# Score blocks in pairs, two fills moved into the written order, and the last output tile in three pieces: one edit to a fused attention and ELU kernel

## The chip, the cores and the metric

The kernel runs on one core of one Trainium2 chip. The metric is device time in microseconds of the whole launch, as the median of several runs. Beside it stands one profiled execution, whose trace gives the times of single instructions from the start of its span. A change of under 0.5% (1.6 us here) can hardly be told from no change.

## The reference

Attention with fixed sparse masks over 8 batches, 8 heads, 576 positions and 64 columns per head, and behind it a two-layer MLP with ELU, all from float32 inputs to a float32 output:

```python
scores = scale * q @ k.T                       # per batch and head, 576 x 576
rel = pos[:, None] - pos[None, :]
local   = (rel >= 0) & (rel < 32)              # heads 0 to 3
strided = (rel >= 0) & (pos % 32 equal)        # heads 4 to 7
attn = softmax(where(mask, scores, -1e9))
x = (attn @ v) as 4608 tokens x 512
h = x @ w_in                                   # 512 -> 2048
g = where(h > 0, h, exp(min(h, 0)) - 1)
out = g @ w_out                                # 2048 -> 512
```

## The kernel before

Positions are dealt out by their remainder modulo 8 (s), so a strided head splits into 8 classes of 72 rows, of which each attends to itself alone; local heads use 6 windows of 96 queries with 128 keys. Tokens keep that order in `xT`, and the stores of the output put them back.

The whole kernel is one list, `ORDER`, written out as a string of some 1380 tokens. Every token calls one small function (the dictionary `run`), which issues a few instructions on one engine. Each engine runs its own instructions in the order of the list, and waits on semaphores for what it needs from others; so the list fixes what stands behind what on each queue. A token is a letter and its arguments, such as `S.2l1.0.12`: batch 2, local heads, pair y = 1, half u = 0, PSUM banks 1 and 2. The eight PSUM banks are also chosen by hand in the tokens. The letters:

- `w` 42 matmuls of zeros (L369); `D` loads by POOL's queue (L230 to L268), which convert float32 to bf16 on the way; `K` casts of the first two strided heads, which SP loads as float32 into `stage` (L375).
- `T` transposes of q or k on PE into a bank for batches 0 and 1 (L388 strided, L391 local), `C`/`c` the copies out of it by ACT or DVE (L399 to L403); `X` a transposing DMA by SP for batches 2 to 7 (L575).
- `S` a score block: 8 (strided) or 6 (local) matmuls with 64-row weights into two banks (L427). `e` its exponential on ACT (L434), `m` the product with the mask on DVE (L441, L447), `O` the product with v, whose extra columns of ones give the sums of the softmax (L490 strided, L497 local; L454 to L475 in batches 0 and 1 with separate matmuls for the sums).
- `n` and `r` logarithm of the sums and exponential of its negative on ACT (L525, L530), `x` the product with it on DVE into `xT` (L555).
- `V` and `W` copies of v on DVE: rows of the previous window (L559), and v of the strided heads between columns of ones (L562).
- `L` the first layer for one 128-row block of h and 512 tokens, four matmuls (L582); in chunk 0 as two halves, `a` (strided heads) and `b` (local heads). `h` exp on ACT (L590), `i` or `j` the clamp to min(e, 1) - 1 on DVE or ACT (L599, L597), `g` the maximum with h on DVE (L610, L608), which also frees the bank.
- `Z` a quarter of the second layer for a tile of 128 tokens, four matmuls (L616). `o` or `q` the copy of the tile to SBUF by ACT or DVE (L622), `t` its two or three stores by SP (L634). The copies share four buffers.
- `Y`/`y` the last tile (7.3) in two halves of 256 columns: matmuls (L642), ACT copies the first half (L655), ACT and DVE share the second (L658, L659); stores by SP and for one piece by ACT.
- `F` fills: the strided mask (`ms`), the window mask (`mk` on POOL, `ml` on DVE).

The order of the work is thus: batch 0's attention, then chunk 0 of the MLP with batch 1's attention among its matmuls, and so on; each chunk of 512 tokens needs the batches that hold them. Before the list runs, SP starts the two `stage` loads, POOL two half loads (qs, ks of batch 0), and DVE clears and fills `zero`, `identity`, `mask_1`, both `vl` tiles, `vsp`, `ones` and the gaps of `kT`.

POOL's loads use eight semaphores in turn, so that the ninth load is issued when the first has landed.

Of the kernel before, what the change touches and what calls it, by code (L numbers as in the profile page):

```python
# [45 lines left out]
D.wo3.0 h.0.1 i.0.7 b.0.0 j.0.11 g.0.7 b.0.6 h.0.0 b.0.12 g.0.10 j.0.1 a.0.15.4 D.qs.2 g.0.11 a.0.9.7
h.0.12 g.0.1 b.0.9 h.0.6 T.1s0.k.2 i.0.12 h.0.9 b.0.15 c.1s0.k a.0.3.1 i.0.6 j.0.9 b.0.3 D.ks.2 g.0.12
h.0.15 T.1l0.k.2 i.0.0 h.0.3 a.0.2.5 g.0.9 C.1l0.k b.0.2 D.vs.2 g.0.6 a.0.5.0 j.0.3 a.0.13.7 g.0.0 h.0.2
b.0.5 j.0.15 g.0.3 b.0.13 j.0.2 g.0.15 S.1s0.1.23 T.1l0.q.6 e.1s0.1 g.0.2 T.1l1.k.1 D.kl.2 T.1l1.q.4
C.1l0.q c.1l1.k S.1s0.0.23 a.0.14.5 h.0.5 m.1s0.1 Z.0.3.0.6 e.1s0.0 c.1l1.q V.1 h.0.13 T.1s1.k.4 i.0.5  # L50
# [657 lines left out]
```

## Time and profile before

| what | value |
|---|---|
| median of 3 runs (lowest, highest) | 315.01 us (314.72, 315.85) |
| the profiled execution | 312.68 us |
| its span, first to last instruction | 310.7 us |
| mean granted TensorE clock | 0.974 |
| PE busy (2330 matmuls) | 299.0 us, 96% |
| ACT busy | 234.5 us, 75% |
| DVE busy | 219.1 us, 71% |
| POOL busy | 79.8 us, 26% |
| loads and stores | 37.59 MB, 121 GB/s mean |

The time of an execution holds some 2 us outside the span. In the profile an engine's line such as "L616 PE MATMUL ... x4" is four instructions of line 616; a bracket behind it is the time that the engine stood idle before and what ended that. PE's durations overlap, so that the distance from one start to the next is what a group costs there. PEld is PE's loading of weights.

### The profile page before, as it was taken

How to read it: one execution, taken by the hardware profiler on the slowest of the kernel's cores; microseconds unless marked ns; L12 is line 12 of the kernel's file. 1: busy time of each engine (PE TensorE's matmuls, PEld its weight loads, DVE VectorE, ACT ScalarE, POOL GpSimd, SP SyncE). 2: the span in 40 equal slices, each digit the busy share in tenths (PEclk: the TensorE clock that was granted, in tenths of full speed). 3: DMA queues.
4: the chain of work that ended last, by engine and by line, in shares of the span. 5: the costliest groups of instructions: out<-in, count | busy, mean ns of one | idle time of the engine just before them, and what ended most of it. 6: DMA issues, size and time to landing. Idle time of an engine off the chain costs nothing.

```text
span 310.7 us, 6213 instructions
## 1 busy us (share of the span) xinstructions
PE 299.0 (96%) x2330; PEld 150.4 (48%) x2330; DVE 219.1 (71%) x422; ACT 234.5 (75%) x421; POOL 79.8 (26%) x107
## 2 busy tenths in 40 slices
...
GB/s 164 188 206 194 207 207 193 165 165 194 165 167 135 129 209 147 133 163 67 126 174 185 122 87 151 169 14 95 36 1 70 0 101 0 37 0 0 40 165 68
DMA packets 106717, 37.59 MB, mean 121 GB/s; under 512 B 88992, under 2 KB 101888, under 8 KB 106688
## 3 DMA queue, kind: packets, MB, share of 16 engines
...
q8 instruction: 18, 0.29, 0.4%
...
## 4 chain that ended last, share of the span: by engine, by line
PE 87%; DVE 4%; ACT 3%; DMA 2%; issue 1%; POOL 1%; ACTq 0%; POOLq 0%
PE ps L616 38%; PE ps L582 38%; PE ps L427 4%; DMA ql<-in_q_dram 2%; PE ps L490 2%; PE ps L497 2%; DVE g L608 1%; PE ps L642 1%; ACT e L434 1%; DVE he L599 1%; DVE g L610 1%; PE ps L391 1%; PE ps L470 1%; ACT ln L525 0%; ACT osb L622 0%
## 5 line engine op out<-in xcount | busy, mean ns | idle before, releaser
L616 PE MATMUL ps<-w_out_sb,g 128*128 128x512 bf16 x560 | 135.6, 380 | 0.0
L582 PE MATMUL ps<-xT,w_in_sb 128*128 128x512 bf16 x576 | 132.0, 379 | 0.0
L590 ACT ACTIVATE he<-ps 128x512 f32<-128x512 f32 x144 | 80.4, 596 | 24.7 <-PE ps L582 24.1
L582 PEld LDWEIGHTS <-w_in_sb 128*128 128x128 bf16 x576 | 54.5, 98 | 63.1 <-issue 0.6
L616 PEld LDWEIGHTS <-g 128*128 128x128 bf16 x560 | 50.4, 98 | 53.8 <-DVE g L610 0.4
L610 DVE TENSOR_TENSOR g<-he,ps 128x512 bf16<-128x512 bf16 x89 | 59.5, 683 | 1.3
L555 DVE TENSOR_TENSOR xT<-ps,ln 64x576 bf16<-64x576 f32 (+1 forms) x64 | 42.9, 678 | 23.9 <-ACT ln L530 22.0
L599 DVE TENSOR_SCALAR he<-he 128x512 bf16<-128x512 f32 x89 | 38.3, 439 | 14.6 <-ACT he L590 13.8
L434 ACT ACTIVATE e<-ps 72x576 bf16<-72x576 f32 (+1 forms) x64 | 39.8, 646 | 7.8 <-PE ps L427 6.8
L525 ACT ACTIVATE ln<-ps 64x576 f32<-64x576 f32 (+1 forms) x64 | 36.7, 582 | 8.3 <-PE ps L497 3.8
L608 DVE SCALAR_TENSOR_TENSOR g<-he,ps 128x512 bf16<-128x512 bf16 x55 | 36.9, 682 | 8.4 <-ACT he L597 8.0
L530 ACT ACTIVATE ln<-ln 64x576 f32<-64x576 f32 (+1 forms) x64 | 39.2, 620 | 1.6
L597 ACT ACTIVATE he<-he 128x512 bf16<-128x512 f32 x55 | 33.8, 628 | 2.7 <-DVE g L610 1.2
L236 POOL DMA_DIRECT2D ql<-in_q_dram x24 | 20.0, 840 | 11.6 <-DMA qTl<-ql 9.6
L441 DVE TENSOR_TENSOR pm<-e,mask_s 72x576 bf16<-72x576 bf16 x32 | 14.4, 449 | 9.6 <-ACT e L434 9.4
L622 ACT COPY osb<-ps 128x512 f32<-128x512 f32 x18 | 10.3, 583 | 13.4 <-PE ps L616 10.4
...
L447 DVE TENSOR_TENSOR pm<-e,mask_l 128x576 bf16<-128x576 bf16 x32 | 14.4, 454 | 6.0 <-ACT e L434 5.6
L622 DVE COPY osb<-ps 128x512 f32<-128x512 f32 x17 | 11.6, 688 | 7.1 <-PE ps L616 6.5
L230 POOL DMA_DIRECT2D vs<-in_v_dram x7 | 4.7, 671 | 39.8 <-DVE vsp L562 38.9
L253 POOL DMA_DIRECT2D vl<-in_v_dram x8 | 10.1, 1259 | 8.0 <-PE ps L497 6.6
L490 PEld LDWEIGHTS <-vsp 72*128 72x128 bf16 x192 | 9.2, 98 | 5.1 <-DVE pm L441 0.2
...
## 6 DMA issues: line engine op xcount, KB each, us to landing
...
```

Of the source, the lines that this page charges most:

```text
L434: nc.scalar.activation(e[0:R], tiles.pop(("S", key, u))[0:R], ACT.Exp, scale=scale)
L525: nc.scalar.activation(t, s_ps, ACT.Ln)
L530: nc.scalar.activation(t, t, ACT.Exp, scale=-1.0)
L555: nc.vector.tensor_mul(dst, o_ps, rc)
L582: nc.tensor.matmul(tiles["h", ch, m], lhsT=w_in_sb[:, c, m * 128:(m + 1) * 128], rhs=xT[:, c, ch * CHUNK:(ch + 1) * CHUNK], start=(c == 2) ...
L590: nc.scalar.activation(e, tiles["h", i[0], i[1]], ACT.Exp)
L597: nc.scalar.activation(e1, e, ACT.Relu, bias=1.0, scale=-1.0)
L599: eng.tensor_scalar(e1, e, scalar1=1.0, scalar2=1.0, op0=ALU.min, op1=ALU.subtract)
L608: nc.vector.scalar_tensor_tensor(dst, e1, -1.0, h, op0=ALU.mult, op1=ALU.max)
L610: nc.vector.tensor_tensor(dst, e1, h, op=ALU.max)
L616: nc.tensor.matmul(ops, lhsT=g[ch % 2][:, m, kk * 128:(kk + 1) * 128], rhs=w_out_sb[:, m, :], start=(m == 0), stop=(m == MC - 1), skip_gro ...
L622: eng(o_sb, tiles.pop(("o", int(ch), int(kk))))
```

## The change

`ORDER` is replaced as a whole: the tokens of the same kinds stand in another order and use other banks. What differs beside place and bank:

- Score blocks (`S`) stand in pairs, one directly behind the other on PE, from batch 2 on: 24 groups of two (30 groups of one to three before). In batches 0 and 1 there are 9 groups (10 before).
- The fill of `vsp` and of the second `vl` tile, which DVE did before the list, become tokens (`F.vp`, `F.v1`).
- The casts of the first strided heads: both of q on ACT, one of k on DVE and one on ACT (both of q on DVE, both of k on ACT before).
- Batch 0: the order of the transposes, of the blocks and of the loads of the weights. The two transposes T.1s1.q and T.1s0.q of batch 1 come later.
- 4 of the 89 clamps of DVE go to ACT; 7 of ACT's 18 output copies go to DVE.
- The last tile in three pieces of 256, 128 and 128 columns; the first copied by ACT, the others by DVE. Tile 8.3 is copied and stored ahead of it, no longer behind it, and tile 7.0 beside its first piece.
- Two small clears more in `kT` (32 columns behind the keys of the local heads).

```diff
 ORDER = """
-w.7.42 D.kl.0 D.ql.0 D.vs.0 K.q.1 D.vl.0 K.q.0 T.0s0.q.7 D.wi2.0 K.k.0 D.qs.1 K.k.1 D.wi1.0 T.0s0.k.6
-c.0s0.k c.0s0.q D.wi3.0 T.0l0.k.5 F.ms T.0s1.k.7 S.0s0.1.01 D.wi0.0 C.0s1.k T.0l1.q.6 e.0s0.1 F.mk
-S.0s0.0.23 C.0l1.q m.0s0.1 T.0l1.k.7 D.kl.1 e.0s0.0 O.0s0.1.41 C.0l1.k m.0s0.0 D.ks.1 T.0l0.q.6 c.0l0.k
-O.0s0.0.70 C.0l0.q F.ml T.0s1.q.3 n.0s0.0 n.0s0.1 S.0l1.1.56 c.0s1.q r.0s0.1 D.vl.1 e.0l1.1 S.0s1.1.01
-V.0 S.0s1.0.23 r.0s0.0 m.0l1.1 S.0l0.1.56 e.0s1.1 e.0l0.1 m.0s1.1 S.0l1.0.01 e.0s1.0 m.0l0.1 S.0l0.0.56
-x.0s0.1 D.ql.1 e.0l1.0 m.0s1.0 O.0l1.1.32 x.0s0.0 e.0l0.0 O.0s1.0.41 n.0l1.1 O.0l0.1.70 m.0l0.0 D.wo0.0
-r.0l1.1 m.0l1.0 O.0s1.1.26 n.0s1.0 x.0l1.1 r.0s1.0 O.0l1.0.51 n.0s1.1 x.0s1.0 r.0s1.1 O.0l0.0.63 n.0l0.1
-x.0s1.1 n.0l1.0 T.1s1.q.4 D.vs.1 T.1s0.q.0 r.0l1.0 c.1s1.q a.0.7.2 n.0l0.0 a.0.11.1 r.0l0.1 a.0.4.4
...
-Z.8.0.2.7 t.7.2 o.7.1 Z.7.0.2.3 t.7.1 Z.7.0.3.3 Z.8.2.2.6 o.7.0 t.7.0 Z.8.0.3.7 Z.8.2.3.6 t.8.1
-Z.8.3.0.5 o.8.2 o.8.0 t.8.2 Z.8.3.1.5 Z.8.3.2.5 t.8.0 Z.8.3.3.5 Y.7.3.0.7 y.7.3.0 Y.7.3.1.6 y.7.3.1
-o.8.3 t.8.3
+w.7.42 D.kl.0 F.vp D.ql.0 F.v1 D.vs.0 k.q.0 F.ms D.vl.0 k.q.1 T.0s0.q.7 D.wi1.0 k.k.0 K.k.1 D.wi0.0
+C.0s0.q T.0s0.k.6 D.wi2.0 T.0s1.k.5 C.0s0.k T.0s1.q.7 D.wi3.0 C.0s1.k S.0s0.0.01 c.0s1.q S.0s0.1.23
+S.0s1.0.45 e.0s0.1 D.qs.1 T.0l0.k.7 e.0s1.0 m.0s0.1 F.mk S.0s1.1.23 m.0s1.0 T.0l1.k.6 e.0s1.1 D.wo0.0
+c.0l0.k T.0l0.q.5 C.0l1.k m.0s1.1 T.0l1.q.4 e.0s0.0 D.ks.1 c.0l1.q O.0s1.1.76 c.0l0.q S.0l1.1.01 m.0s0.0
+O.0s1.0.54 F.ml e.0l1.1 S.0l0.1.23 n.0s1.1 m.0l1.1 S.0l1.0.01 n.0s1.0 r.0s1.1 D.ql.1 V.0 O.0s0.0.64
+e.0l1.0 x.0s1.1 e.0l0.1 m.0l1.0 S.0l0.0.01 n.0s0.0 m.0l0.1 O.0l1.0.73 e.0l0.0 O.0s0.1.42 r.0s0.0 D.kl.1
+r.0s1.0 x.0s0.0 O.0l1.1.10 n.0s0.1 m.0l0.0 n.0l1.0 O.0l0.1.62 x.0s1.0 r.0s0.1 r.0l1.0 O.0l0.0.53 x.0s0.1
+n.0l1.1 x.0l1.0 a.0.5.4 n.0l0.0 D.wo1.0 n.0l0.1 r.0l0.0 a.0.1.7 r.0l1.1 x.0l0.0 r.0l0.1 a.0.0.5 x.0l0.1
+a.0.3.0 x.0l1.1 a.0.2.6 D.wo2.0 b.0.2 a.0.4.3 h.0.2 b.0.4 j.0.2 b.0.1 b.0.3 h.0.4 g.0.2 b.0.0 h.0.1
+i.0.4 D.wo3.0 a.0.8.2 h.0.3 b.0.5 i.0.3 a.0.6.6 h.0.5 g.0.3 a.0.15.1 D.vl.1 h.0.0 b.0.6 i.0.5 j.0.1
...
+S.2l1.0.12 S.2l1.1.56 x.2s0.1 Z.1.1.0.0 e.2l1.0 e.2l1.1 X.kl.3 m.2l1.0 S.2l0.0.12 S.2l0.1.34 m.2l1.1
+e.2l0.0 O.2l1.0.56 W.3 Z.1.1.1.0 e.2l0.1 m.2l0.0 O.2l1.1.12 n.2l1.0 m.2l0.1 Z.1.0.1.7 D.qs.4 n.2l1.1
+D.ql.3 Z.1.1.2.0 r.2l1.0 r.2l1.1 O.2l0.0.34 x.2l1.0 Z.1.1.3.0 n.2l0.0 x.2l1.1 O.2l0.1.56 r.2l0.0
+Z.1.0.2.7 n.2l0.1 x.2l0.0 D.ks.4 r.2l0.1 q.1.1 S.3s0.0.12 S.3s0.1.34 D.vs.4 Z.1.0.3.7 e.3s0.1 x.2l0.1
+D.vl.3 e.3s0.0 m.3s0.1 S.3s1.0.34 S.3s1.1.56 O.3s0.1.01 e.3s1.1 L.2.6.2 n.3s0.1 m.3s1.1 q.1.0 L.2.9.6
+X.qs.4 r.3s0.1 m.3s0.0 h.2.6 L.2.7.7 x.3s0.1 e.3s1.0 D.kl.4 i.2.6 L.2.3.5 h.2.7 m.3s1.0 g.2.6 h.2.9
+O.3s0.0.01 L.2.1.4 h.2.3 i.2.7 i.2.9 X.ql.3 n.3s0.0 i.2.3 L.2.4.3 g.2.9 r.3s0.0 L.2.10.2 g.2.3 h.2.1
...
+g.8.9 Z.8.1.1.3 Z.8.2.1.7 Z.8.0.1.6 L.7.14.5 Z.8.1.2.3 h.7.14 j.7.14 Z.8.0.2.6 g.7.14 Z.8.3.0.0
+Z.8.2.2.7 Z.8.3.1.0 Z.8.2.3.7 Z.7.2.1.1 q.8.2 Z.7.1.2.4 t.8.2 Z.8.1.3.3 Z.7.1.3.4 o.8.1 t.8.1 Z.8.0.3.6
+q.7.1 Z.7.0.1.2 q.8.0 Z.7.2.2.1 t.8.0 Z.7.2.3.1 t.7.1 Z.8.3.2.0 q.7.2 Z.8.3.3.0 t.7.2 Z.7.0.2.2 q.8.3
+Z.7.0.3.2 t.8.3 Y.7.3.0.7 o.7.0 t.7.0 y.7.3.0 Y.7.3.1.6 y.7.3.1 Y.7.3.2.5 y.7.3.2
...
 
 
@@ -305,16 +305,18 @@
             w[:, 0:n * D].rearrange("p (n w d) -> p n w d", w=2, d=D // 2)[:, :, 0, :], two)
         nc.vector.memset(w[:, n * D:], two)
 
-    for t in vl_t:
+    def fill_vloc(t):
         fill_ones(t, HG * LB)
         nc.vector.memset(blocks(t, HG * LB)[0:PRE, 0, :], 0.0)
-    fill_ones(vs_p, HG * NS)
+
+    fill_vloc(vl_t[0])
 
     nc.vector.memset(ones, 1.0)
     for t in kT:
         nc.vector.memset(t["s"][:, NS * RS:KSY], 0.0)
         nc.vector.memset(t["s"][:, KSY + NS * RS:], 0.0)
         nc.vector.memset(t["l"][:, 0:PRE], 0.0)
+        nc.vector.memset(t["l"][:, S:S + PRE], 0.0)
 
     def fill(what):
         if what == "ms":
@@ -323,6 +325,10 @@
             nc.vector.tensor_scalar(eq, same, scalar1=0, scalar2=None, op0=ALU.is_equal)
             nc.vector.scalar_tensor_tensor(mask_s, dist, float(RS), eq, op0=ALU.is_ge,
                                            op1=ALU.mult)
+        elif what == "vp":
+            fill_ones(vs_p, HG * NS)
+        elif what == "v1":
+            fill_vloc(vl_t[1])
         elif what == "mk":
             nc.gpsimd.affine_select(
                 mask_1, mask_1, compare_op=ALU.is_ge, fill=0.0,
@@ -369,11 +375,10 @@
             nc.tensor.matmul(ps[:, int(bank), 384:512], lhsT=zero, rhs=zero, start=True, stop=True,
                              skip_group_check=True)
 
-    def cast(nm, x):
+    def cast(eng, nm, x):
         i, x = "qk".index(nm), int(x)
         f = NS * D
-        (nc.vector.tensor_copy if nm == "q" else nc.scalar.copy)(
-            raw[nm + "s"][0:RS, x * f:(x + 1) * f],
+        eng(raw[nm + "s"][0:RS, x * f:(x + 1) * f],
             stage[0:RS, (2 * i + x) * f:(2 * i + x + 1) * f])
 
     def transposes(key, nm, bank):
@@ -635,32 +640,31 @@
             c, i = c + n, i + 1
 
 
-    def l2_half(ch, kk, i, bk):
-        f = d_model // 2
-        ops = tiles["o", ch, kk, i] = ps[:, int(bk), 0:f]
+    def piece(i):
+        f = d_model // 4
+        return (0, 2 * f) if i == "0" else ((1 + int(i)) * f, (2 + int(i)) * f)
+
+    def l2_piece(ch, kk, i, bk):
+        f0, f1 = piece(i)
+        ops = tiles["o", ch, kk, i] = ps[:, int(bk), 0:f1 - f0]
         for m in range(MC):
             nc.tensor.matmul(
                 ops, lhsT=g[int(ch) % 2][:, m, int(kk) * 128:(int(kk) + 1) * 128],
-                rhs=w_out_sb[:, m, int(i) * f:(int(i) + 1) * f],
+                rhs=w_out_sb[:, m, f0:f1],
                 start=(m == 0), stop=(m == MC - 1), skip_group_check=True)
 
-    def out_half(ch, kk, i):
-        f = d_model // 2
+    def out_piece(ch, kk, i):
+        f0, f1 = piece(i)
         if i == "0":
             tiles["osb", ch, kk] = p_osb.tile([128, d_model], F32, tag="osb", name="osb")
         o_sb = tiles["osb", ch, kk]
-        o_ps = tiles.pop(("o", ch, kk, i))
-        c0, h = int(i) * f, f // 2
-        if i == "0":
-            nc.scalar.copy(o_sb[:, 0:f], o_ps)
-            store(ch, kk, (nc.sync,), slice(0, f))
-        else:
-            nc.scalar.copy(o_sb[:, f:f + h], o_ps[:, 0:h])
-            nc.vector.tensor_copy(o_sb[:, f + h:], o_ps[:, h:])
-            store(ch, kk, (nc.sync, nc.scalar), slice(f, d_model))
+        (nc.scalar.copy if i == "0" else nc.vector.tensor_copy)(
+            o_sb[:, f0:f1], tiles.pop(("o", ch, kk, i)))
+        store(ch, kk, (nc.sync,) if i == "0" else (nc.sync, nc.scalar), slice(f0, f1))
 
     run = {
-        "w": warm, "K": cast, "T": transposes, "F": fill,
+        "w": warm, "K": lambda nm, x: cast(nc.vector.tensor_copy if nm == "q" else nc.scalar.copy, nm, x),
+        "k": lambda nm, x: cast(nc.scalar.copy if nm == "q" else nc.vector.tensor_copy, nm, x), "T": transposes, "F": fill,
         "c": lambda *a: copy_T(nc.vector.tensor_copy, *a),
         "C": lambda *a: copy_T(nc.scalar.copy, *a),
         "S": scores, "e": exp_s, "m": mask, "O": pv, "n": log_sums, "r": recip, "x": write_x,
@@ -668,7 +672,7 @@
         "a": lambda ch, m, bk: l1(ch, m, (2, 3), bk), "b": lambda ch, m: l1(ch, m, (0, 1)),
         "L": lambda ch, m, bk: l1(ch, m, (2, 3, 0, 1), bk), "h": exp_h,
         "i": lambda *a: clamp(nc.vector, *a), "j": lambda *a: clamp(nc.scalar, *a),
-        "g": elu, "Z": l2, "t": store, "Y": l2_half, "y": out_half,
+        "g": elu, "Z": l2, "t": store, "Y": l2_piece, "y": out_piece,
         "o": lambda *a: copy_o(nc.scalar.copy, *a),
         "q": lambda *a: copy_o(nc.vector.tensor_copy, *a),
     }
```

More of the change, by code (lines that the diff above doesn't have):

```diff
@@ L46 @@
[L46 to L50, printed above, removed]
```

177 lines of the change are left out of this document (86 added, 91 removed).

## The prediction

> **What bounds the kernel now.** I read the page first, then the busy time by stage, then PE's timeline.
>
> ```profile
> span 310.7 us, 6213 instructions
> ...
> GB/s 164 188 206 194 207 207 193 165 165 194 165 167 135 129 209 147 133 163 67 126 174 185 122 87 151 169 14 95 36 1 70 0 101 0 37 0 0 40 165 68
> ...
> PE 87%; DVE 4%; ACT 3%; DMA 2%; issue 1%; POOL 1%; ACTq 0%; POOLq 0%
> ```
> ```profile
> 0.00:22.26 22.26, 16.90 (x282) 14.19 (x283) 13.23 (x45) 13.66 (x27) 16.01 (x26) 0.69 1.20 186
> 22.26:305.06 282.80, 282.09 (x2054) 136.16 (x2050) 205.55 (x377) 220.01 (x392) 63.76 (x81) 1.00 0.87 117
> 305.06:310.70 5.64, 0.00 (x0) 0.00 (x0) 0.29 (x1) 0.85 (x2) 0.00 (x0) 0.78 0.31 89
> ```
> PE carries 87% of the chain that ended last. The windows (length, busy time of PE, PEld, DVE, ACT, POOL, granted clock, DMA share, GB/s) show three stages: 22.26 us until the first L582 matmul, at a mean clock of 0.69; 282.80 us in which PE pauses for 0.7 us in all; and 5.64 us after PE's last matmul. So an edit is worth what it takes out of PE's own order in the middle, and what it shortens at the ends. The sum is 22.26 + 282.80 + 5.60 = 310.7 us. The profiled execution took 312.68 us; the median of the runs is 315.01, 2.3 us above it. I subtract the difference in span from the median.
>
> **Middle: what a score block costs PE.** Here a block stands alone and then two stand together.
>
> ```profile
> 140.97 1.03 PE L616 MATMUL ps<-w_out_sb,g 128*128 128x512 bf16 x4
> 141.92 0.30 PE L427 MATMUL ps<-qTl,kTl 64*128 64x96 bf16 x6
> 142.16 1.04 PE L616 MATMUL ps<-w_out_sb,g 128*128 128x512 bf16 x4
> 143.13 0.43 PE L427 MATMUL ps<-qTl,kTl 64*128 64x96 bf16 x12
> 143.49 1.04 PE L616 MATMUL ps<-w_out_sb,g 128*128 128x512 bf16 x4
> 144.36 0.42 PE L497 MATMUL ps<-pm,vl 128*128 128x96 bf16 x6
> 144.62 1.02 PE L616 MATMUL ps<-w_out_sb,g 128*128 128x512 bf16 x4
> ```
> ```profile
> PEld L427 <- issue: 15.5, 38, 0.6
> ```
> Go by starts, since durations overlap. Four L616 matmuls take 0.87 us (143.49 to 144.36) when no score block follows, and 0.95 to 0.97 (140.97 to 141.92; 142.16 to 143.13) when one does. A block alone takes 0.24, two take 0.36. So the first block of a group costs about 0.10 ahead + 0.24 = 0.34, each further one 0.125: a merged block saves **0.215 us**. The wait row says why: the weight load stands for about 0.4 us before 38 groups, when PE goes from 128-row to 64-row weights, and not within a group.
>
> I counted groups in both orders. From the first L582 on the old order has 37 groups of score blocks, the new one 28. Nine fewer x 0.215 = -1.94 us. Two transposes of batch 1 (T.1s1.q, T.1s0.q) stood before the first L582 and now come after: 2 x 8 matmuls, +0.51 (0.26 each, as six L497 matmuls take from 144.36 to 144.62). All other matmuls are the same in number and shape, but for the last tile (below).
>
> **What may come late in the new order.** A pair gives ACT two exponentials at once. The old order lost time in the same way twice:
>
> ```profile
> 61.61 0.31 PE L427 MATMUL ps<-qTs,kTs 64*128 64x72 bf16 x8 [0.26 <-DVE g L610]
> ...
> 88.23 0.87 PE L427 MATMUL ps<-qTs,kTs 64*128 64x72 bf16 x24
> ```
> ```profile
> 96.35 0.69 DVE L610 TENSOR_TENSOR g<-he,ps 128x512 bf16<-128x512 bf16 x1
> 96.95 0.68 DVE L608 SCALAR_TENSOR_TENSOR g<-he,ps 128x512 bf16<-128x512 bf16 x1
> 97.55 0.42 DVE L599 TENSOR_SCALAR he<-he 128x512 bf16<-128x512 f32 x1
> 98.00 0.69 DVE L610 TENSOR_TENSOR g<-he,ps 128x512 bf16<-128x512 bf16 x1
> ```
> Three blocks took 0.87 instead of 0.55: about 0.3 us for a bank; 0.3 also at 61.6. Both go. I compared, for each bank and each product that PE reuses, the PE time between maker and user with the work that the order puts between them on ACT and DVE. Two places are short. (1) S.2l1.0 to S.3s1.0: ACT has 13 operations of about 0.6 in 8.3 us of PE time, in a chain with waits: 0.3 us. (2) L.2.5.6 to L.2.0.6: PE has 3.1 us between them, DVE one x, four g and three or four clamps, by these rows 0.75 + 4 x 0.60 + 3 x 0.34 = 4.2 less what it was ahead: 0.8 us. Elsewhere the distances are like the old ones that cost nothing. So 0.6 lost before, 1.1 after: **+0.5**, between 0 (DVE is ahead) and 3 (each of a dozen tight places costs 0.2). The four clamps moved to ACT and seven output copies moved to DVE stay under that cover.
>
> Loads (POOL) and transposing DMAs (SP) move too. By PE time in the orders, batches 2 to 7 have at least 7.1 us from a load's place to its transposition in the old order, 6.3 in the new, and 5.3 and 11.0 from there to the first score. A transposition that waits for its load holds the stores behind it on SP, and so one of four output buffers; at the shortest places (qs.4, ks.4, ks.6) the next output copies come over 8 us later. No cost, with the middle's bounds.
>
> Middle: 282.80 - 1.94 + 0.51 + 0.5 = 281.9.
>
> **Start.**
>
> ```profile
> 9.24 0.69 PE L391 MATMUL ps<-identity,kl 72*64 72x72 bf16 x16 [2.03 <-DMA kl<-in_k_dram]
> ...
> 11.04 0.69 PE L391 MATMUL ps<-identity,ql 72*64 72x72 bf16 x16 [0.16 <-DMA ql<-in_q_dram]
> ...
> 21.62 0.81 PE L388 MATMUL ps<-identity,xT 72*128 72x72 bf16 x16
> 22.26 2.11 PE L582 MATMUL ps<-xT,w_in_sb 128*128 128x512 bf16 x9
> ```
> ```profile
> 5.71 1.14 ACT L375 CAST ks<-g 72x512 bf16<-72x512 f32 x2 [3.62 <-DMA g<-in_k_dram]
> ...
> 11.09 0.65 ACT L434 ACTIVATE e<-ps 72x576 bf16<-72x576 f32 x1
> ...
> 16.21 3.13 ACT L434 ACTIVATE e<-ps 72x576 bf16<-72x576 f32 x5
> ```
> ```profile
> L530 ACT ACTIVATE ln<-ln 128x288 f32<-128x288 f32 x16 | 6.7, 439 | 0.3
> L525 ACT ACTIVATE ln<-ps 128x288 f32<-128x288 f32 x16 | 5.9, 402 | 0.6 <-PE ps L454 0.5
> ```
> ```profile
> 7.00:8.00 1.00, 0.21 (x4) 0.08 (x3) 0.76 (x3) 0.00 (x0) 1.00 (x3) 0.95 1.20 193
> ...
> 21.00:22.00 1.00, 1.00 (x20) 0.67 (x16) 0.68 (x2) 0.97 (x4) 0.52 (x1) 0.73 1.30 224
> ```
> The old order puts the transposition of kl third on PE; it waits until 9.24 for kl, and the third strided transposition and all scores queue behind it: first exponential at 11.09. Now four strided transpositions come first, and the key casts run side by side on ACT and DVE (one each, from 5.71) instead of 1.14 us on ACT. The fills vp and v1 run on DVE before its cast, done by about 5 (0.9 us each, as in the old order), under the wait for the keys. Casts done at 6.3, transposes and copies to 8.7, scores 8.1 to 9.2, first exponential about 8.9. Three more and a copy follow (to 12.2); then the local scores need ql at 11.04, two transposes at half clock (1.2), copies (0.4) and a PV block: next exponential at 13.65. From there to the last strided reciprocal ACT has 4 exponentials (five took 3.13, so 0.63 each, at best 0.55 where none waits), five logarithms (0.40 alone) and four reciprocals (0.44 alone), which start 0.30 to 0.38 apart where they follow one another: 5.0 to 5.8 us, and DVE's product of 0.45: first L582 at 19.4 to 20.0. Two L582 blocks in, bank 5 is not free until about 21.1; and the clock, which falls at 7.9 and rises at 21.54 (0.95 and 0.73 are means of 1 and 0.5), is still half, so those blocks take twice their time and hide that wait. In terms of a full-clock start this is **20.6** instead of 22.26: -1.7. Bounds: 20.1 (clock up one stage earlier) and 22.3.
>
> A rule of the Trainium skill, "TensorE: Matmul & The Clock Gate", section on the clock gate, says that the clock is decided in free-running windows of about 3.4 us. By it the low stretch is four windows (21.54 - 7.9 = 13.6; the trace agrees), and the pause at bank 5 may cost one window more.
>
> **Tail.**
>
> ```profile
> 305.09 0.27 ACT osb L658
> ...
> 305.39 0.30 DVE osb L659
> ...
> 305.71 0.55 ACTq L634
> ...
> 306.36 0.58 ACT osb L622
> ```
> ```profile
> 303.79 3.92 SPq L634 DMA_DIRECT2D out_dram<-osb  x5
> ```
> After PE's end come two copies one behind the other, a store on ACT, only then the copy of tile 8.3 (0.58) and its two stores on SP, until 307.71; the span ends 2.95 later. In the new order tile 8.3 is copied and stored while PE still works, and one DVE copy of 128 columns is last: 0.03 + 0.29 + 0.02 + 0.55 (ACT's store, SP's beside it; SP's queue is free at PE's end, 11 stores of 0.35 to 0.5 in the last 5 us) = 0.9, + 2.95 = 3.85 instead of 5.60: **-1.75**. Bounds 3.6 and 4.5. The last tile's matmuls take the same time in three pieces as in two (as many columns; L497's 96 columns run at 43 ns a matmul, so the weight load does not bound a smaller piece), bounds 0 and +0.3.
>
> **Sum:** 20.6 + 281.9 + 3.85 = 306.35, -4.3 us; **310.7 us**.
>
> **Rivals.**
> - *The clock comes up one window later.* For: PE pauses near 21. Against: half-rate matmuls fill the pause. 3.4 us at half rate, +1.7: 312.4.
> - *Pairing does not do what it says.* The second block waits for its bank, so the 1.94 turn into waiting, or the dozen tight places cost 2.5 us: 312.8 to 313.5. For: ACT is busy 220.01 of 282.80 us and gets two exponentials at once. Against: the old order's three-block groups, all but one, took 0.125 per further block.
> - *Slower: the vector queue stops for a load.* W.2 (copy of vs.2, L562) is now ahead of the last masks and products of batch 1 on DVE. Loads land one after another:
>
> ```profile
> 15.09 1.54 POOL L253 DMA_DIRECT2D vl<-in_v_dram  x1 [1.05 <-DMA vl<-in_v_dram]
> ...
> 24.41 0.75 POOL L268 DMA_DIRECT2D w_out_sb<-in_moe_w_out_dram  x1 [2.29 <-DMA w_in_sb<-in_moe_w_in_dram]
> 26.82 0.74 POOL L268 DMA_DIRECT2D w_out_sb<-in_moe_w_out_dram  x1 [1.66 <-DMA w_in_sb<-in_moe_w_in_dram]
> ```
> ```profile
> 47.12 1.94 SPq L575 DMA_TRANSPOSE qTs<-qs  x1
> ```
> POOL goes on when a load has landed: two weight quarters 2.4 us apart. vl.0 lands by 15, qs.2 by 47.1 (its transposition starts then); the new order moves the same loads up to there, and vs.2 right behind (1.7 us for 320 KB): 48.7. DVE reaches W.2 near 49.9. It decides from 1.2 us of lateness. At the 165 GB/s of the eighth slice instead of the 201 that the third to seventh average, the 34 us from vl.0 to vs.2 become 41.5: 7.5 late, 6.3 of it PE time: 317.0. Against: that stage ran at 193 to 207 until 54 us before.
>
> **How the numbers follow.** The forecast as worked out, 309.0 to 312.0: 0.62. Clock window: 0.10. Pairing or new waits: 0.18. Slower by W.2: 0.06. Faster than 309: 0.04. The range 309.0 to 313.5 takes in the bounds of start, waits and tail and leaves out about 0.17. 0.5% (what a measurement tells from no change) is 1.6 us: below 313.4 lie 0.85, within 0.10, above 316.6 0.05.
>
> **What would show it.** The L427 weight loads wait for issue in 31 to 33 groups instead of 38; the first L582 before 20.5; first exponential near 9; PE's last matmul near 302.5, 3.9 us before the end. I am wrong if PE has gaps near 50 us or in batches 2 to 4 of over 2 us in all, or if the clock rises after 22.

## The result and the profile after

The new kernel takes **310.21 us** (median of 4 runs, 308.9 to 310.66), the kernel before 314.87 in the runs beside it; the ratio is 0.9844 [0.9803, 0.9885]. The whole interval lies below 1, so the new kernel is faster, by 1.6%; the time is 0.5 us below the forecast of 310.7. The profiled execution of the new kernel took 310.66 us, with a span of 308.7. Most line numbers of the new kernel are higher by 5: scores L432, first layer L587 (L582 before), second layer L621, stores L639, last tile L651 and L661.

First the page of the new kernel (span, busy time, chain that ended last), then its busy time by the three stages, with the columns as before: length, busy time of PE, PEld, DVE, ACT and POOL, granted clock, DMA share, GB/s.

```profile
span 308.7 us, 6270 instructions
...
PE 298.1 (97%) x2346; PEld 150.8 (49%) x2346; DVE 222.2 (72%) x427; ACT 232.1 (75%) x418; POOL 79.6 (26%) x107
...
PE 77%; DVE 9%; ACT 6%; DMA 3%; issue 2%; POOL 1%; DVEq 0%; POOLq 0%; ACTq 0%
```
```profile
0.00:20.53 20.53, 15.35 (x266) 13.16 (x267) 12.84 (x45) 13.42 (x27) 13.82 (x24) 0.75 1.19 182
20.53:304.23 283.70, 282.74 (x2081) 137.65 (x2080) 209.11 (x382) 218.72 (x392) 65.74 (x83) 0.99 0.92 119
304.23:308.73 4.50, 0.00 (x1) 0.00 (x0) 0.29 (x1) 0.00 (x0) 0.00 (x0) 0.82 0.19 49
```

Two things are to be seen. The two ends became shorter (22.26 to 20.53, and 5.64 to 4.50), and the middle did not: 283.70 instead of 282.80. And the spans of the two profiled executions differ by 2.0 us, the medians by 4.7. Both have to be explained, so the first experiment is a second profile of each kernel.

### The profile page after: what moved, and what is told of

It reads as the page before. It is cut to its first block, busy times and chain, and to the rows that moved or that the text cites. A ratio compares the mean times of both kernels' runs of the same rounds, so it can differ in the third digit from the quotient of the medians.

```text
span 308.7 us, 6270 instructions
## 1 busy us (share of the span) xinstructions
PE 298.1 (97%) x2346; PEld 150.8 (49%) x2346; DVE 222.2 (72%) x427; ACT 232.1 (75%) x418; POOL 79.6 (26%) x107
## 4 chain that ended last, share of the span: by engine, by line
PE 77%; DVE 9%; ACT 6%; DMA 3%; issue 2%; POOL 1%; DVEq 0%; POOLq 0%; ACTq 0%
PE ps L621 36%; PE ps L587 31%; DMA vs<-in_v_dram 3%; PE ps L432 3%; DVE g L615 3%; DVE he L604 2%; ACT e L439 2%; DVE g L613 2%; PE ps L502 2%; PE ps L495 2%; ACT he L595 1%; ACT ln L535 1%; PE ps L651 1%; ACT ln L530 1%; DVE xT L560 1%
## 5 line engine op out<-in xcount | busy, mean ns | idle before, releaser
L621 PE MATMUL ps<-w_out_sb,g 128*128 128x512 bf16 x560 | 133.4, 379 | 0.1
L587 PE MATMUL ps<-xT,w_in_sb 128*128 128x512 bf16 x576 | 132.7, 382 | 0.5 <-DVE g L615 0.5
L587 PEld LDWEIGHTS <-w_in_sb 128*128 128x128 bf16 x576 | 55.1, 98 | 65.0 <-issue 2.8
L621 PEld LDWEIGHTS <-g 128*128 128x128 bf16 x560 | 50.9, 98 | 55.2 <-DVE g L613 0.9
L615 DVE TENSOR_TENSOR g<-he,ps 128x512 bf16<-128x512 bf16 x85 | 56.7, 682 | 1.6
L613 DVE SCALAR_TENSOR_TENSOR g<-he,ps 128x512 bf16<-128x512 bf16 x59 | 39.6, 682 | 19.4 <-ACT he L602 19.1
L439 ACT ACTIVATE e<-ps 72x576 bf16<-72x576 f32 (+1 forms) x64 | 39.1, 646 | 14.9 <-PE ps L432 12.9
L604 DVE TENSOR_SCALAR he<-he 128x512 bf16<-128x512 f32 x85 | 36.2, 433 | 4.3 <-ACT he L595 3.4
L602 ACT ACTIVATE he<-he 128x512 bf16<-128x512 f32 x59 | 36.4, 636 | 1.0 <-DVE g L615 0.3
L627 DVE COPY osb<-ps 128x512 f32<-128x512 f32 x24 | 16.5, 686 | 10.7 <-PE ps L621 8.7
L627 ACT COPY osb<-ps 128x512 f32<-128x512 f32 x11 | 6.5, 586 | 14.1 <-PE ps L621 7.6
L230 POOL DMA_DIRECT2D ks<-in_k_dram x7 | 4.7, 674 | 29.4 <-DMA kTs<-ks 27.4
```

Of the source, the lines that this page charges most:

```text
L439: nc.scalar.activation(e[0:R], tiles.pop(("S", key, u))[0:R], ACT.Exp, scale=scale)
L587: nc.tensor.matmul(tiles["h", ch, m], lhsT=w_in_sb[:, c, m * 128:(m + 1) * 128], rhs=xT[:, c, ch * CHUNK:(ch + 1) * CHUNK], start=(c == 2) ...
L602: nc.scalar.activation(e1, e, ACT.Relu, bias=1.0, scale=-1.0)
L604: eng.tensor_scalar(e1, e, scalar1=1.0, scalar2=1.0, op0=ALU.min, op1=ALU.subtract)
L613: nc.vector.scalar_tensor_tensor(dst, e1, -1.0, h, op0=ALU.mult, op1=ALU.max)
L615: nc.vector.tensor_tensor(dst, e1, h, op=ALU.max)
```

## The experiments

**The two kernels once more.** Nothing is edited.

> The old kernel once more. Theory (when the granted clock falls and rises at the start differs from one execution to the next, and with it the time): first L582 matmul at 22.0 to 22.6 as before, but the clock's rise may lie elsewhere than at 21.54, each us of half clock after the first L582 costing 0.5. Rival (the clock follows the instructions alone): fall at 7.9 and rise at 21.5 again, and the middle stage 282.8.

> The new kernel once more. Theory: the rise of the clock (23.8 in the first profile, after the first L587 at 20.5) may come 1 to 3 us sooner or later; the stage without the half-rate matmuls stays at 282.1, the tail at 4.5. Also whether the load of vs lands at 14.0 again and holds PE until then. Rival: all as in the first profile, within 0.2.

Measured: the kernel before 314.24 us, the new one 310.2. The stages of the kernel before in this execution, then of the new one:

```profile
0.00:23.09 23.09, 17.17 (x282) 14.43 (x283) 13.60 (x45) 13.94 (x28) 15.97 (x26) 0.67 1.19 185
23.09:306.65 283.56, 279.69 (x2015) 136.43 (x2049) 205.19 (x377) 219.75 (x392) 64.01 (x81) 1.00 0.87 116
306.65:312.27 5.62, 0.00 (x1) 0.00 (x0) 0.29 (x1) 0.85 (x2) 0.00 (x0) 0.92 0.31 89
```
```profile
0.00:20.15 20.15, 16.55 (x266) 14.50 (x267) 12.86 (x45) 13.39 (x27) 13.92 (x25) 1.00 1.20 186
20.15:303.78 283.63, 278.50 (x2042) 137.30 (x2080) 209.75 (x382) 218.74 (x392) 65.84 (x83) 1.00 0.93 119
303.78:308.30 4.52, 0.00 (x1) 0.00 (x0) 0.29 (x1) 0.00 (x0) 0.00 (x0) 0.88 0.19 49
```

The new kernel nearly repeats itself: PE's last matmul ends at 304.23 and 303.78. The kernel before doesn't: 305.06 and 306.65. (In these two traces 37 and 39 matmul records are missing, and the second has no record of a lower clock, though its matmuls of the start are as long as at half rate, 0.45 us for eight L468 matmuls as in the first profile; so its PE busy time and its clock are not read.) What differs in the old order is the clock. These are one-microsecond windows of the second profile of the kernel before and of the same start in the experiment with tile 8.3 below; the share of full speed stands third from the end:

```profile
7.00:8.00 1.00, 0.18 (x4) 0.05 (x2) 0.78 (x3) 0.00 (x0) 1.00 (x2) 0.82 1.23 192
24.00:25.00 1.00, 1.00 (x4) 0.37 (x4) 0.95 (x3) 0.76 (x2) 0.47 (x1) 0.65 1.24 206
```
```profile
8.00:9.00 1.00, 0.00 (x0) 0.00 (x0) 0.93 (x4) 0.00 (x0) 1.00 (x3) 0.67 1.25 203
25.00:26.00 1.00, 1.00 (x5) 0.42 (x4) 0.17 (x1) 0.00 (x0) 0.17 (x1) 0.79 1.25 208
```

The first pair belongs to the second profile, the other to the experiment; the rows of the first profile (0.95 at 7, 0.73 at 21) stand in the prediction. A mean of 0.82 between 1 and 0.5 means that the clock fell at 7.64, and 0.65 that it rose at 24.70. So the low stretch lasted from 7.90 to 21.54 in the first profile (13.64 us), but from 7.64 to 24.70 (17.06) and from 8.34 to 25.42 (17.08) in the two others. The difference is 3.4 us each time. The profile on which the forecast was built was the short case, and two of three traces of the old start are the long one. What this makes of the median is taken up at the end of the next section.

**Pairs undone.** One block of each of the 24 pairs of batches 2 to 7 goes one PE token earlier, so that it stands alone. The first pair, as an example:

```diff
-L.1.12.6 h.1.1 g.1.4 X.ql.2 h.1.7 S.2s0.0.01 S.2s0.1.34 i.1.1
+S.2s0.0.01 L.1.12.6 h.1.1 g.1.4 X.ql.2 h.1.7 S.2s0.1.34 i.1.1
```

> The new kernel with each of the 24 pairs of batches 2 to 7 split by one PE group, all else in its order. Theory (a merged block saves 0.215 us, paid as weight loads that wait for issue): 24 groups more, 24 x 0.215 = +5.2 us against the new kernel, from the first L587 matmul to PE's last; about 50 waits for issue of L432's weight loads instead of 26; the time comes back to about the old one (315). Rival (the pairs themselves bring nothing, the gain is start and tail): within 1 us of the new kernel, 309 to 311.

Measured: 317.31 us, 1.0075 [1.0047, 1.0104] of the kernel before, so 7.1 more than the new kernel. PE's weight loads before score blocks, in the new kernel and in this one (total wait, groups, longest):

```profile
PEld L432 <- issue: 10.8, 26, 0.4
```
```profile
PEld L432 <- issue: 21.5, 51, 0.5
```

25 groups more stand 10.7 us longer for their weight load, 0.43 each. What a group costs PE is less, as its timeline shows by the starts:

```profile
80.53 0.30 PE L432 MATMUL ps<-qTl,kTl 64*128 64x96 bf16 x6 [0.43 <-DVE xT L560]
80.76 1.04 PE L621 MATMUL ps<-w_out_sb,g 128*128 128x512 bf16 x4
81.73 0.30 PE L432 MATMUL ps<-qTl,kTl 64*128 64x96 bf16 x6
```

A block alone takes 0.23 here, and the four L621 matmuls ahead of the next one take 0.97 instead of 0.87: 0.33 in all, as in the old order. A pair takes 0.46 in the new kernel by the same measure, so a merge is worth 0.20, close to the forecast's 0.215, and 24 groups more are 4.8 to 5.2 us. The other 2 us of the 7.1 are put down to new waiting, of which the first row is an example: a block that was moved forward stands 0.43 us for the product on DVE that frees its bank. The price of a group is thus confirmed by the starts; that the rest is waiting alone is not shown. The rival that pairs bring nothing (309 to 311) is refuted.

**Tile 8.3 alone.** The kernel before, with the copy and the stores of tile 8.3 ahead of the last tile:

```diff
-Z.8.3.3.5 Y.7.3.0.7 y.7.3.0 Y.7.3.1.6 y.7.3.1 o.8.3 t.8.3
+Z.8.3.3.5 o.8.3 t.8.3 Y.7.3.0.7 y.7.3.0 Y.7.3.1.6 y.7.3.1
```

> The old kernel, with the copy and stores of tile 8.3 placed ahead of the last tile. Theory (the old tail was long because this copy and its two stores queue behind the last tile's on ACT and SP): PE's end to the span's end 4.1 to 4.5 us instead of 5.64, so -1.1 to -1.5 us on the old time (313.5). Rival (the landing of the last store sets the end, whatever comes before it): 5.4 to 5.7, time as before.

Measured: 312.75 us, 0.992 [0.989, 0.995], 1.8 less than the kernel before beside it (314.58). The last stage of its trace:

```profile
307.22:311.07 3.85, 0.00 (x0) 0.00 (x0) 0.29 (x1) 0.27 (x1) 0.00 (x0) 1.00 0.23 59
```

The place of one tile takes the tail from 5.62 to 3.85, below the 4.1 to 4.5 that were expected and the whole of what the forecast gave to the new tail. So the three pieces must cost something, since with them the tail is 4.50.

**Two halves again, in the new kernel.** The last tile goes back to two halves, the second copied half by ACT and half by DVE; tile 8.3 stays ahead of it.

```diff
-Y.7.3.0.7 o.7.0 t.7.0 y.7.3.0 Y.7.3.1.6 y.7.3.1 Y.7.3.2.5 y.7.3.2
+Y.7.3.0.7 o.7.0 t.7.0 y.7.3.0 Y.7.3.1.6 y.7.3.1
-"Y": l2_piece, "y": out_piece
+"Y": l2_half, "y": out_half
```

> The new kernel with the last tile in two halves as before, tile 8.3 still ahead of it. Theory (what shortened the tail is tile 8.3's place; three pieces save one copy of 0.27 in a chain and are paid back by SP's wait for a semaphore): tail 4.0 to 4.5 us, within 0.5 us of the new kernel. Rival (the pieces carry the gain of the tail): 5.0 to 5.6, +0.5 to +1.1 us.

**ACT's stores in the last piece only.** In the new kernel with its three pieces, SP stores both halves of piece 1, and ACT takes part in the last piece only:

```diff
-store(ch, kk, (nc.sync,) if i == "0" else (nc.sync, nc.scalar), slice(f0, f1))
+store(ch, kk, (nc.sync, nc.scalar) if i == "2" else (nc.sync,), slice(f0, f1))
```

> The new kernel with both stores of the last tile's second piece on SP. Theory (SP's last store waits 1.1 us for the semaphore of the store that ACT has just issued): SP's last issue starts at most 1.2 us after PE's end instead of 1.53, tail 3.9 to 4.2 us instead of 4.49, -0.3 to -0.6 us. Rival (the tail is the landing of the stores alone): 4.4 to 4.6.

Measured: 308.33 us with the halves, 0.9811 [0.9792, 0.983], tail 3.80, again less than the 4.0 to 4.5 expected; 309.83 with the other stores, 0.9868 [0.9835, 0.99], tail 4.22, at the upper end of what was expected. The queues that issue the last stores, in the new kernel; beside them what SP waited for after 304:

```profile
304.59 0.48 ACTq L639 DMA_DIRECT2D out_dram<-osb  x1
305.76 0.47 SPq L639 DMA_DIRECT2D out_dram<-osb  x1
```
```profile
SPq L639 <- DMA out_dram<-osb: 1.1, 1, 1.1
SPq L639 <- DVE osb L661: 0.5, 1, 0.5
```

And in the kernel with two halves:

```profile
302.20 2.43 SPq L639 DMA_DIRECT2D out_dram<-osb  x3
...
304.17 0.56 ACTq L639 DMA_DIRECT2D out_dram<-osb  x1
```

In the new kernel the last copy is done at 304.56 and ACT issues its half of the last piece at once. SP stands 1.1 us more, for a DMA: the store that ACT issued at 303.70 for the piece before, to which the trace gives the same semaphore as to SP's last store. SP issues that store only at 305.76, is done with it at 306.23, and the span ends 2.5 us later. With two halves ACT issues one store only and SP waits for the copy alone; the last issue is over at 304.73, and the span ends 2.6 later. With the last pieces' stores dealt out otherwise, SP waits for the copy alone (0.5 us), but has one store more in its row. So by these traces the third piece costs 0.7 us of tail, and the place of tile 8.3 is the whole gain there.

**The start: two scores ahead.** In the first profile of the new kernel PE stands still at its first product with v, and ACT with it:

```profile
14.04 0.45 PE L468 MATMUL ps<-pm,vs 72*64 72x72 bf16 x8 [1.73 <-DMA vs<-in_v_dram]
14.42 0.42 PE L432 MATMUL ps<-qTl,kTl 64*128 64x96 bf16 x6
```
```profile
8.46 1.89 ACT L439 ACTIVATE e<-ps 72x576 bf16<-72x576 f32 x3
...
14.88 0.65 ACT L439 ACTIVATE e<-ps 128x576 bf16<-128x576 f32 x1 [3.46 <-PE ps L432]
```

O.0s1.1 waits for the load vs until 14.0, and the first local score block stands behind it. In the edit, S.0l1.1 and S.0l0.1 and their exponentials go ahead of it:

```diff
-O.0s1.1.76 c.0l0.q S.0l1.1.01 m.0s0.0 O.0s1.0.54 F.ml e.0l1.1 S.0l0.1.23
+c.0l0.q S.0l1.1.01 S.0l0.1.23 e.0l1.1 m.0s0.0 F.ml e.0l0.1 m.0l1.1 O.0s1.1.76 O.0s1.0.54
```

> The new kernel; in batch 0 the first two local score blocks and their exponentials stand ahead of the first PV block, which waits for the load of vs. Theory (PE stands at that wait with the local scores queued behind it, and ACT's chain behind them sets the start): next exponential at 12.8 to 13.2 instead of 14.88, first L587 1.0 to 1.8 us earlier (19 to 19.5); of that 0.5 to 1.5 us are left at the end, because the clock may still be at half rate there: 308.7 to 309.7. Rival (the strided products need vs anyway and set the start): first L587 at 20.3 to 20.6, time as the new kernel's 310.2.

Measured: 309.38 us, 0.9846 [0.9821, 0.9871]: no gain that can be told from the new kernel's 0.9844. ACT's timeline with the edit, and PE's stages:

```profile
13.41 1.19 ACT L439 ACTIVATE e<-ps 128x576 bf16<-128x576 f32 x2 [0.93 <-PE ps L432]
```
```profile
0.00:20.12 20.12, 15.34 (x267) 13.33 (x268) 13.10 (x45) 13.61 (x27) 13.83 (x24) 0.71 1.19 185
```

The exponential comes 1.5 us earlier, the first hidden tile 0.4 (20.12 against 20.53), with vs landing at the same time (13.92). The rest of the step is not gained, and the chain that ended last shows why: it now starts from another load.

```profile
5.14 10.64 DMA vl<-in_v_dram
```

vl, with v of the local heads, lands at 15.78; DVE's copy V.0, a product, a mask, the last local exponential and the logarithms follow it up to the first hidden tile. A third load stands behind these two. The second hidden tile needs quarter 0 of the first weights, which landed between 19.56 and 20.77 in the ten traces of the new start. Where vs came early, PE stood there, as in the experiment with ACT's stores in the last piece only:

```profile
18.77 1.01 PE L587 MATMUL ps<-xT,w_in_sb 128*128 128x512 bf16 x2
20.17 3.17 PE L587 MATMUL ps<-xT,w_in_sb 128*128 128x512 bf16 x10 [0.38 <-DMA w_in_sb<-in_moe_w_in_dram]
```

So by these traces an earlier first tile is worth little with this order of loads.

**The start: matmuls of zeros in PE's waits.** 6, 10 and 24 matmuls of zeros at three places where PE waits:

```diff
-C.0s0.q T.0s0.k.6
+C.0s0.q w.3.6 T.0s0.k.6
...
-c.0l0.k T.0l0.q.5
+c.0l0.k w.4.10 T.0l0.q.5
...
-c.0l1.q O.0s1.1.76
+c.0l1.q w.2.24 O.0s1.1.76
```

> The new kernel with 40 more matmuls of zeros in PE's three waits of the start (6, 10 and 24; they add nothing to the output). Theory (the clock falls because PE is not busy enough between 6 and 10, and rises late because of the wait at 12 to 14): the clock stays up or rises before 20.5, and the 1.6 us that the first four L587 blocks lose at half rate go: -1.0 to -2.0 us, 308.2 to 309.2. Rival (the clock's stretches do not follow such fillers, or the fillers delay the blocks behind them): within 0.5 of 310.2, or up to 1 us longer.

Measured: 310.27 us, 0.9888 [0.9866, 0.991]. The clock in the stretches that matter:

```profile
18.00:19.00 1.00, 0.52 (x10) 0.41 (x10) 1.00 (x3) 1.00 (x5) 0.00 (x0) 0.95 1.23 199
22.00:23.00 1.00, 1.00 (x5) 0.44 (x4) 0.21 (x1) 0.00 (x0) 0.23 (x1) 0.84 1.26 210
```

With the zeros the clock stayed up until 18.90. It then fell for 3.42 us, to 22.32, and that stretch lies on the first hidden tiles (from 19.61). The full rate before it was not free either: the 24 zeros kept PE from 11.62 to 13.06, though vs had landed at 12.44, and they stand in the chain that ended last with 1.45 us. So part of what transposes, scores and products gained was spent on zeros, and the tiles ran at half rate as before.

**The start: fills and casts as before.** In the new kernel the two fills come first on DVE, and the first casts go to the engines that had them before.

```diff
-w.7.42 D.kl.0 F.vp D.ql.0 F.v1 D.vs.0 k.q.0 F.ms D.vl.0 k.q.1 T.0s0.q.7 D.wi1.0 k.k.0 K.k.1 D.wi0.0
+F.vp F.v1 w.7.42 D.kl.0 D.ql.0 D.vs.0 K.q.1 F.ms D.vl.0 K.q.0 T.0s0.q.7 D.wi1.0 K.k.0 K.k.1 D.wi0.0
```

> The new kernel with the fills vp and v1 first on DVE and the first casts on the engines of the kernel before (both of q on DVE, both of k on ACT). Theory: the start now ends at the wait of the first strided PV block for load vs (landed 11.6 to 14.0 in five profiles of the new order), not at the casts: the key casts take 1.1 us on ACT instead of 0.7 side by side, the first exponential comes 0.3 to 0.6 later than 8.46, and the first L587 matmul stays at 20.0 to 20.6 if vs lands by 14; total 310.2, within 0.4. Rival: the placed fills and split casts carry the earlier start, so that the first exponential comes near 9.5 and the first L587 matmul 0.8 to 1.0 later; total 311.0.

Measured: 308.74 us, 0.982 [0.9782, 0.9858]. ACT's first strided exponential:

```profile
9.21 1.18 ACT L439 ACTIVATE e<-ps 72x576 bf16<-72x576 f32 x2 [0.35 <-PE ps L432]
```

It comes 0.75 us later than in the new kernel (8.46), but the first L587 matmul comes at 19.13. vs landed at 12.27 here; so it did in the experiment with the pairs undone, which has the new fills and casts and its first L587 matmul at 19.02. In that comparison the placed fills and the split casts are worth 0.1 us, against 0.8 to 1.0 by the rival. That this kernel is faster than the new one is not shown, since the intervals overlap.

**The start undone as a whole.** The new kernel with batch 0 as in the kernel before: the two fills, then the old order from its first token to c.1s1.q, then the new order without what was done. Some of the first hidden tiles change places for the sake of their banks. The first lines and the place of the splice:

```diff
-w.7.42 D.kl.0 F.vp D.ql.0 F.v1 D.vs.0 k.q.0 F.ms D.vl.0 k.q.1 T.0s0.q.7 D.wi1.0 k.k.0 K.k.1 D.wi0.0
+F.vp F.v1 w.7.42 D.kl.0 D.ql.0 D.vs.0 K.q.1 D.vl.0 K.q.0 T.0s0.q.7 D.wi2.0 K.k.0 D.qs.1 K.k.1 D.wi1.0
...
-n.0l1.1 x.0l1.0 a.0.5.4 n.0l0.0 D.wo1.0 n.0l0.1 r.0l0.0 a.0.1.7 r.0l1.1 x.0l0.0 r.0l0.1 a.0.0.5 x.0l0.1
-a.0.3.0 x.0l1.1 a.0.2.6 D.wo2.0 b.0.2 a.0.4.3 h.0.2
+T.1s1.q.4 D.vs.1 T.1s0.q.0 r.0l1.0 c.1s1.q a.0.5.4 C.1s0.q n.0l0.0 x.0l1.0 D.wo1.0 r.0l0.1 a.0.0.5 r.0l0.0
+x.0l0.1 a.0.3.0 a.0.4.3 x.0l0.0 a.0.1.7 a.0.2.6 D.wo2.0 b.0.2 h.0.2
```

> The new kernel with batch 0 of the kernel before: its order up to the copy of T.1s1.q, its first casts, the two fills ahead of the list, and T.1s1.q and T.1s0.q of batch 1 again ahead of the first hidden tile; from there the new order, the first five hidden tiles in another sequence so that their banks are free. So the start alone is undone; pairs and tail stay new. Theory (the forecast's step): the start is worth 1.7 us in terms of the full clock, 0.5 of it given back by the two transposes, so this kernel takes 1.2 us more than the new one: 311.4 against 310.2, ratio to the kernel before 0.988, PE's end about 305.2. Rival: the new start brings the first hidden tile 2 us earlier but into the half-rate stretch of the clock, so that nothing is left of it; then this kernel takes 310.2 or a little less, ratio 0.983 to 0.985, with PE's end near 304.

Measured: 316.64 us, 1.0074 [1.0048, 1.0099]: far more than either theory gave. PE's timeline shows why:

```profile
22.85 0.59 PE L587 MATMUL ps<-xT,w_in_sb 128*128 128x512 bf16 x1
26.60 3.67 PE L587 MATMUL ps<-xT,w_in_sb 128*128 128x512 bf16 x10 [3.17 <-DMA w_in_sb<-in_moe_w_in_dram]
```

The old start loads the quarters of the first weights in the order 2, 1, 3, 0; the second of the new hidden tiles needs quarter 0, which landed last, at 26.55. So the splice added a wait of its own: 3.17 us in the row, some 2.9 by the starts, since PE's weight loads show one matmul more before it than the row has. The clock's windows in this kernel:

```profile
8.00:9.00 1.00, 0.02 (x2) 0.03 (x2) 0.73 (x4) 0.00 (x0) 1.00 (x2) 0.93 1.22 195
29.00:30.00 1.00, 1.00 (x5) 0.45 (x4) 0.00 (x0) 0.00 (x0) 0.17 (x1) 0.83 2.34 163
```

It fell at 8.86 and stayed low until 29.34, for 20.48 us, with that wait in between. The experiment is confounded. PE's last matmul ended at 309.68; less the 2.9 it is 306.8, or 2.6 to 3.0 later than in the two profiles of the new kernel. That speaks for a start that is worth more than nothing, but it is an estimate and not a measurement.

**The wait near 100 us.** Tile 5 of chunk 2 earlier on DVE, and L.2.0.6 ahead of O.3s1.1 on PE:

```diff
-g.2.10 O.3s1.0.01 L.2.15.4 n.3s1.0 i.2.5 i.2.2 t.1.3 O.3s1.1.23 r.3s1.0 g.2.5 g.2.2 h.2.12 L.2.0.6
+i.2.5 g.2.5 O.3s1.0.01 L.2.15.4 n.3s1.0 g.2.10 i.2.2 t.1.3 L.2.0.6 O.3s1.1.23 r.3s1.0 g.2.2 h.2.12
```

> The new kernel, with the DVE work of hidden tile 5 of chunk 2 (its clamp and its product) ahead of a score block's neighbours, and L.2.0.6 on PE ahead of O.3s1.1. The new kernel's PE stands 0.70 us near 100 us, at L.2.0.6 (0.5 of it at L587 for the product L615 of DVE). Theory: this is DVE's queue, as forecast; with the product two places earlier and the taker of the bank one block earlier or level, the pause at that place falls to 0.1 to 0.3 and no other of over 0.3 us appears in the next 8 us; PE's end 0.4 to 0.6 us earlier than it would be, total 309.6 against 310.2 for the new kernel. Rival: DVE is behind as a whole in that stretch, so the same 0.5 to 0.7 us only move to the next PV block or hidden tile; total 310.2.

Measured: 309.18 us, 0.9829 [0.9791, 0.9867]. PE's timeline around the place:

```profile
100.06 0.42 PE L495 MATMUL ps<-pm,vsp 72*128 72x72 bf16 x8
100.86 3.66 PE L587 MATMUL ps<-xT,w_in_sb 128*128 128x512 bf16 x16 [0.37 <-DVE g L615]
104.82 1.47 PE L621 MATMUL ps<-w_out_sb,g 128*128 128x512 bf16 x6 [0.30 <-DVE g L613]
```

The eight matmuls of 100.06 need 0.26, so 0.54 is lost there, and another 0.5 before 104.82. In the new kernel the same stretch loses 0.70 and 0.24. The wait has moved, as the rival said, and in both kernels it is DVE's products that PE waits for. The time alone can't decide between 309.6 and 310.2, since the two intervals overlap.

**Three edits together.** Scores ahead, tile 5 earlier, last tile in two halves.

```diff
-O.0s1.1.76 c.0l0.q S.0l1.1.01 m.0s0.0
+c.0l0.q S.0l1.1.01 S.0l0.1.23 e.0l1.1 m.0s0.0 F.ml e.0l0.1 m.0l1.1 O.0s1.1.76
...
-X.ql.4 h.2.2 g.2.10 O.3s1.0.01 L.2.15.4 n.3s1.0 i.2.5
+X.ql.4 h.2.2 i.2.5 g.2.5 O.3s1.0.01 L.2.15.4 n.3s1.0 g.2.10
...
-Y.7.3.1.6 y.7.3.1 Y.7.3.2.5 y.7.3.2
+Y.7.3.1.6 y.7.3.1
```

> The new kernel with three edits of the experiments together: the two local score blocks ahead of the first strided PV block, tile 5 of chunk 2 earlier on DVE, and the last tile in two halves as before the change (tile 8.3 stays ahead of it). If the gains add: tail 3.8 (0.7 less), the pause near 100 us 0.4 less, the second local exponential 1 us earlier at the start but only 0 to 0.7 of it in PE's end: 308.0 to 308.6 beside 310.2 for the new kernel (ratio to the kernel before 0.979 to 0.982). Rival: the two halves alone gave 308.3, and what the other two save is given back to the half-rate stretch of the clock or to the next wait: 308.3, no better than the halves.

Measured: 308.98 us, 0.982 [0.9792, 0.9849]. It is no better than the halves alone (0.9811 [0.9792, 0.983]), so the rival holds. The best version is the new kernel with the last tile in two halves. It beats the kernel before clearly; its lead over the new kernel rests on the tail, 3.80 instead of 4.50 in the traces, while the two intervals overlap.

## Why the prediction was right, point by point

The time was hit, but in part by luck. The terms that concern the pairs were right; the gains of the two ends were forecast too large, and the way from the trace to the median made up for it.

**Pairing: right.** Behind the first hidden tile PE's trace has 37 groups of score blocks before and 28 after, as counted. By the starts a group of one costs 0.33, of two 0.46, of three 0.59, so the nine groups less are worth 1.8 us (forecast 1.94). Undoing the pairs gave the price once more. Only the sign to look for was loose: weight loads wait in 26 groups, not 31 to 33.

**New waits: right, at their places.** PE's timeline of the new kernel at the two places, and how DVE's copy W.2 stands on its queue:

```profile
88.56 0.73 PE L432 MATMUL ps<-qTs,kTs 64*128 64x72 bf16 x16
...
90.20 0.43 PE L432 MATMUL ps<-qTs,kTs 64*128 64x72 bf16 x16
...
100.90 0.42 PE L495 MATMUL ps<-pm,vsp 72*128 72x72 bf16 x8
101.86 4.48 PE L587 MATMUL ps<-xT,w_in_sb 128*128 128x512 bf16 x20 [0.54 <-DVE g L615]
```
```profile
51.97 0.68 DVE L567 COPY vsp<-vs 72x2048 bf16<-72x2048 bf16 x1
```

The first pair takes 0.73 where one without a wait takes 0.43: 0.30, at S.3s0.0 (forecast 0.3, one pair later). Eight L495 matmuls take 0.96 where 0.26 is their slot: 0.70 (forecast 0.8). Added up over all places of the middle where a start at full clock is over 0.08 us late, the waits are 1.8 us, in the kernel before 1.3: +0.5, as forecast. With the half-rate loss of 1.6 us that is worked out below, the terms of the middle come to -1.8 + 0.5 + 0.5 + 1.6 = +0.8, and +0.9 was measured.

**The slower rival did not come.** W.2 runs at 51.97 with no idle time ahead of it. Its load had landed at 48.97, close to the forecast's 48.7, and DVE came 2 us later than the forecast's 49.9. There were 3.0 us to spare.

**The start: the step "next exponential at 13.65" failed.** The first exponential came at 8.46 (forecast 8.9). But the forecast let the local scores wait for ql alone and left out what stands ahead of S.0l1.1 on PE's queue, a product with v that waits for vs. That load landed at 13.99 here, and at 11.6 to 13.9 in the other traces of the new start. So the next exponential came at 14.88, and the first hidden tile at 20.53 and 20.15 instead of 19.4 to 20.0. The two loads behind it, vl and quarter 0 of the weights, have no term in the forecast either; by the experiments they leave little to win from an earlier vs.

**The start: the clock's rise as a fixed time failed as well.** Two windows of the new kernel:

```profile
10.00:11.00 1.00, 0.14 (x8) 0.10 (x6) 1.00 (x3) 1.00 (x3) 0.87 (x3) 0.56 1.21 196
...
23.00:24.00 1.00, 1.00 (x4) 0.39 (x3) 0.14 (x1) 0.00 (x0) 0.66 (x1) 0.62 1.26 208
```

The clock fell at 10.12 and rose at 23.76, again 13.64 us, but 2.2 later than the forecast took from the old trace. The first four tiles at half rate lost 1.6 us, so that this start is worth 22.1 and not 20.6 in terms of the full clock. That is close to the first rival, though the stretch is not one window longer but the same four windows, later. The Trainium skill, "TensorE: Matmul & The Clock Gate", Part 1, says that the windows are free-running, 3.4 us long, and not tied to the start of a kernel; the traces agree (13.64, 17.06, 20.48 and 3.42 us are four, five, six and one of 3.41). What the half rate costs in PE's end is less clear. PE's timeline of the new kernel's second profile has tiles at the full rate there:

```profile
20.15 1.19 PE L587 MATMUL ps<-xT,w_in_sb 128*128 128x512 bf16 x3
21.78 7.07 PE L587 MATMUL ps<-xT,w_in_sb 128*128 128x512 bf16 x32 [0.44 <-DVE xT L560]
29.17 1.02 PE L587 MATMUL ps<-xT,w_in_sb 128*128 128x512 bf16 x4 [0.33 <-DVE g L615]
```

The first tile began 0.4 earlier, the next ones waited for `xT` and banks instead, and PE ended only 0.45 earlier. So in this trace half-rate tiles would have covered other waits. The eight traces of the paired order and the new start that record the clock speak for a higher price, though each but the first has an edit of its own: with the rise at 20.9 and 21.1 PE ended at 302.4 and 302.6, with the rise at 23.8 at 304.2, and the five in between at 303.1 to 303.9.

**The tail: the step "SP's beside it; SP's queue is free" failed.** 4.50 instead of 3.85. SP's queue was free, but its store waits for the store that ACT had issued before. The gain was 1.1 instead of 1.75, and the three pieces have no part in it.

**Why the sum was right all the same.** The forecast for PE's end was 302.5, and it came at 304.23 and 303.78; with the tail, the span was 308.7 and 308.3 instead of 306.35, 2.0 to 2.4 too much. The median was hit because the forecast took the trace's difference from a median that lay 2.3 above the profiled execution, as if the new kernel had the same gap. It hasn't: its profiled executions (310.66 and 310.2) are at its median of 310.21. That two errors of some 2 us cancel is luck. The rows above point to the window more in which the old order's clock is low, in two of its three traces; the traces of the new start that record a clock have four windows, or one with the zeros. The mean granted clock of each execution bears this out. Of 40 executions of the kernel before that were timed beside the experiments and recorded a lower clock, 36 had a mean of 0.963 to 0.972 and took 313.73 to 316.01 us; four had 0.974 to 0.977, like the 0.974 of the forecast's profile, and took 312.35 to 313.58. So that profile was of a rare, short kind. The medians of the two kinds lie 1.3 us apart, so this explains part of the 2.3; that the window is the cause, and what makes the rest, is not shown.
